# Loading k and q of the first two blocks as one pair of neighbouring tokens, in an attention and MLP kernel

## The chip, the cores and the metric

The kernel runs on one core of a Trainium2 chip. The metric is the device time of one launch in microseconds (us). Five things work side by side on a core: TensorE (PE in the profile, its weight loads PEld), VectorE (DVE), ScalarE (ACT), GpSimd (POOL) and SyncE (SP). SP, ACT and POOL also start transfers; the tables call those queues SPq, ACTq and POOLq.

## The reference

Attention with a sliding window of 128 keys and a bias that grows with distance, for 8 batches, 8 heads, 576 tokens, head size 64. Its result, seen as 4608 tokens of 512 features, goes through a two-layer MLP with squared ReLU.

```python
scores = scale * np.matmul(q, k.transpose(0, 1, 3, 2))
mask = (rel >= 0) & (rel < window)             # window = 128
scores = np.where(mask, scores + bias[None], -1000000000.0)
attn = np.exp(scores - np.max(scores, axis=-1, keepdims=True))
attn = attn / (np.sum(attn, axis=-1, keepdims=True) + 1e-09)
x = np.matmul(attn, v).transpose(0, 2, 1, 3).reshape(B * S, H * D)   # (4608, 512)
h = x @ w_in                                   # w_in (512, 2048)
out = np.maximum(h, 0.0) ** 2 @ w_out          # w_out (2048, 512)
```

## The kernel before

**Tiling.** Each batch of 576 tokens is cut into five blocks, four of 128 tokens and one of 64, so that there are 40 blocks, numbered through. A block goes through these steps: load k, q, v; turn k and q (transposes `tp` on PE, copied into a tile `kqT`); scores `ps_s` on PE; exponentials `E` on ACT (L598); the product with the masks, `P`, on DVE (L609); the values `pv` on PE (L639); the division on DVE (L662, L672), which gives `x`; the turn of `x` (`xp`, L698), copied into `xT`. From block 12 on (13 for `x`) the turns are DMA transposes.

The MLP takes groups of 512 tokens. Group 0 and group 1 use plain products `h` (L745), group 0 in four quarters of 128 tokens, the others a fast scheme of seven products in place of eight with sums of weights and tokens (`f`, L820; `o`, L979). `weight_sums` (L383 to L394) makes the sums of `w_in` that the scheme needs, in 32 DVE instructions of 256 columns.

**Order.** Nothing is ordered by hand. Each step is a task with an estimated duration for one or more engines, a key, its dependencies and the buffers that it takes and frees. `Plan.order` goes through all tasks as a list scheduler does and fixes which engine does which task and in what order. `SPREAD` shifts the keys of groups of tasks by random draws with fixed seeds, so that each list of draws gives another order of the whole program. Where the plan sees PE idle in its first 14 us, the last lines put small matmuls on `ident` there (L1127, L1129), which compute nothing that is used.

**The loads at the start.** All of k, q, v, w_in and w_out comes through POOL's queue, converted to bfloat16 on the way; `FIRST` (L221) gives the order: `b0` is the k, q, v of block 0, `i0` a quarter of the columns of w_in, `o0` a quarter of the rows of w_out. Only k and q of block 0 go another way (`load_block`, L405 to L424): as float32 into tiles `raw`, in halves of four heads, k by SP and q by ACT, one token a partition, so that a piece of 64 numbers (256 bytes) stands together in memory. A copy (`cast`) then converts each half. `prepare` turns block 0 in halves too: two transposes each of k and of q, and a copy of 256 columns after each two; the first half of block 0's scores (heads 0 to 3) needs only the first half of both.

Of the kernel before, what the change touches and what calls it, by code (L numbers as in the profile page):

```python
# [9 lines left out]
FP32 = mybir.dt.float32  # L10
BF16 = mybir.dt.bfloat16
# [190 lines left out]
def kernel(  # L202
    ctx: ExitStack, tc: tile.TileContext, q, k, v, moe_w_in, moe_w_out, out
):
    nc = tc.nc

    B, H, S, D = q.shape
# [10 lines left out]
    NG = NT // 512  # L218
    NBLK = B * NKB

    FIRST = "b0 b1 b2 i0 i1 b3 i2 b4 b5 i3 b6 o0 b7 b8 o1 o2 b9 o3"  # L221
    SPLIT = ([(0, 128), (128, 256), (256, 384), (384, 512)], [(0, 256), (256, 512)])

    KQ_DMA, X_DMA = 12, 13
# [158 lines left out]
    def weight_sums(n, key):  # L383
        w = w_in_sb.rearrange("p (c k) (j r f) -> p c r k j f", c=2, r=2, f=128)
        a11, a12, a21, a22 = (w[:, c, r, :, 2 * n:2 * n + 2] for r in range(2) for c in range(2))
        s1, s2, s3, s4 = (w_sum[:, i, :, 2 * n:2 * n + 2] for i in range(4))
        last = None
        for o, a, b, op in ((s1, a21, a22, ALU.add), (s2, s1, a11, ALU.subtract),
                            (s3, a11, a21, ALU.subtract), (s4, a12, s2, ALU.subtract)):
            def emit(o=o, a=a, b=b, op=op):  # L390
                for k in range(2):
                    nc.vector.tensor_tensor(o[:, k], a[:, k], b[:, k], op=op)
# [5 lines left out]
    def load_block(m, key):  # L398
        b, kb = divmod(m, NKB)
        n = blk[kb]  # L400
        s_in[m, "k"] = s_in[m, "q"] = Slot("kq")
        s_in[m, "v"] = Slot("v")
        for i, (nm, src) in enumerate((("k", k), ("q", q), ("v", v))):
            sl = s_in[m, nm]
            if m == 0 and nm != "v":  # L405
                st = Slot("osb")
                t_in[m, nm] = []
                for hf in range(2):
                    cols = slice(hf * 256, hf * 256 + 256)

                    def raw(src=src, st=st, nm=nm, hf=hf, cols=cols):
                        if not hf:
                            st.tile = work.tile([128, 512], FP32, tag="osb", bufs=plan.bufs["osb"], name="raw")
                        (nc.sync if nm == "k" else nc.scalar).dma_start(
                            st.tile[:, cols].rearrange("s (h d) -> s h d", d=D),
                            src[b, 4 * hf:4 * hf + 4, 0:n, :].rearrange("h s d -> s h d"))

                    def cast(i=i, st=st, sl=sl, nm=nm, hf=hf, cols=cols):
                        copy(t_in[0, nm][hf], kq[sl.idx][:, i, cols], st.tile[:, cols])
                    t_raw = plan.add({"SP" if nm == "k" else "ACT": 450.0}, -2e6 + hf, raw, [], [st],  # L420
                                     lat=(2490.0 if nm == "k" else 2860.0) + 650.0 * hf)
                    t_in[m, nm].append(plan.add({"DVE": 270.0, "ACT": 300.0}, key + 0.1 * hf + 0.01 * i, cast,
                                                [t_raw], [sl], [st]))
                continue  # L424

            def emit(i=i, src=src, sl=sl, nm=nm):
                o = (vt[sl.idx][0:n, :, 0:D] if nm == "v"
                     else (kq[sl.idx][0:n, i] if n == 128 else kq[sl.idx][i * n:i * n + n, 0]).rearrange("s (h d) -> s h d", h=H))
                nc.gpsimd.dma_start(o, src[b, :, kb * 128:kb * 128 + n, :].rearrange("h s d -> s h d"))  # L429
            t_in[m, nm] = load(key + 0.01 * i, 920.0 if n == 128 else {"k": 550.0, "q": 300.0, "v": 550.0}[nm], emit, [t_ones] + (t_zeros if m >= NKB - 1 else []) if nm == "v" else [], [sl])  # L430

    for i, what in enumerate(FIRST.split()):
        {"b": load_block, "i": load_w_in, "o": load_w_out}[what[0]](int(what[1:]), -9e5 + i)
    for m in range(2 * NKB, NBLK):
        load_block(m, -5e5 + m)

# [4 lines left out]
    def copy(task, o, i):  # L441
        if task.eng == "DVE":
            nc.vector.tensor_copy(o, i)
        else:
            nc.scalar.activation(o, i, AF.Copy)

    def prepare(m):
# [5 lines left out]
        kq_by_dma = m >= KQ_DMA  # L453


        sk = sk_of[m] = Slot("kqT")
        if kq_by_dma:
            def turn_kq():
                src = kq[s_in[m, "k"].idx]
# [251 lines left out]
    m = 0  # L711
# [246 lines left out]
    def product(g, i, key):  # L958
# [13 lines left out]
        for j, x in ([(j, x) for x in range(len(parts)) for j in range(FCB // 2)] if halves  # L972
                     else [(j, x) for j in range(FCB // 2) for x in range(len(parts))]):
                t, lo, hi = parts[x]

                def emit(j=j, x=x, t=t, lo=lo, hi=hi):
                    if opens and j == 0 and (x == 0 or apart):
                        bank[x].tile = bank_tile(bank[x], "o")
                    nc.tensor.matmul(bank[x].tile[:, t * 256 + lo:t * 256 + hi],  # L979
                                     left(g, what, j)[:, t * 128:(t + 1) * 128], right(by, j)[:, lo:hi],  # L980
                                     start=opens and j == 0 and (x == 0 or apart), stop=j == FCB // 2 - 1,
                                     skip_group_check=True)
                t = x
                new = j == 0 and t == 0
                here = [bank[t]] if opens and j == 0 and (t == 0 or apart) else []
                end = i == 6 and j == FCB // 2 - 1 and t == len(parts) - 1
                if what[0] == "s":
                    needs = [t_sum[g, j // 4]]
                else:
                    needs = [q for lo, hi, q in g_sq[g][2 * j + (what != "a11")]]  # L990
                last = plan.add({"PE": mm(hi - lo)}, key(i * 16 + 2 * j + min(t, 1)), emit,
                                [last, (t_wmix if by[0] == "t" else t_wout)[j // 2], kp["t"][where] if new else None] + needs,
                                here, [g_slots[g], s_slots[g][0]] if end else [s_slots[g][1]] if i == 1 and j == FCB // 2 - 1 and t == 1 else [])
                if j == FCB // 2 - 1:
                    done_at.append(last)
# [166 lines left out]
```

## Time and profile before

| what | us |
|---|---|
| median of three runs (lowest, highest) | 291.88 (290.7, 292.52) |
| the profiled execution's own time | 291.28 |
| its span, first to last instruction | 289.4 |
| PE busy in the span | 281.4 |
| DVE busy | 256.4 |
| ACT busy | 228.8 |
| POOL busy | 107.7 |

The span is what the views of the profile divide up; the 1.88 us beyond it lie outside the instructions. The time of a launch is read against the median. The granted TensorE clock was 1.00 throughout. PE is busy 97% of the span, so what is looked for is the 8 us in which it isn't, and matmuls that do nothing useful.

### The profile page before, as it was taken

The numbers are of one execution on the slowest core, as the hardware profiler recorded it, in microseconds if no ns is written. First come the engines' busy times: TensorE is split into PE (matmuls) and PEld (weight loads), VectorE is DVE, ScalarE is ACT, GpSimd is POOL, SyncE is SP. The second block draws the span as 40 slices with busy tenths as digits, with TensorE's granted clock in tenths as the row PEclk, the third lists the DMA queues.
The fourth block names the chain that finished last, engine by engine and source line by source line (L and its number), as shares of the span: only waits on it lengthen the run. The fifth ranks groups of instructions, "written<-read, shape, count | busy, mean of one in ns | idle before, by whom it ended". The sixth has DMA issues, their size and how long they took to land.

```text
span 289.4 us, 9511 instructions
## 1 busy us (share of the span) xinstructions
PE 281.4 (97%) x3879; PEld 239.5 (83%) x3885; DVE 256.4 (89%) x627; ACT 228.8 (79%) x470; POOL 107.7 (37%) x134
## 2 busy tenths in 40 slices
PE   8899999999999999999999999999999999999995
PEld 6788878865788888888888898888888888888894
DVE  6867779999798999998999999989999988998823
ACT  6659788995489985999899989898879888588420
POOL 8958676844644437322734245332000000000000
PEclk9999999999999999999999999999999999999999
DMA  9999999999999999999999999999234111201223
GB/s 135 161 181 162 173 177 180 155 137 178 173 155 151 187 176 179 153 170 126 209 145 137 138 198 139 162 170 179 35 100 72 46 21 59 88 0 39 74 75 109
DMA packets 166011, 38.36 MB, mean 133 GB/s; under 512 B 153040, under 2 KB 165456, under 8 KB 165968
## 3 DMA queue, kind: packets, MB, share of 16 engines
q0 software_dynamic: 114704, 18.10, 91.0%
q1 hardware_dynamic: 50208, 19.41, 37.6%
q8 instruction: 30, 0.49, 0.7%
q10 hardware_dynamic: 1056, 0.26, 0.4%
q14 instruction: 13, 0.11, 0.1%
HBM read 36.70 MB, written 9.44 MB: 159 GB/s over the span
## 4 chain that ended last, share of the span: by engine, by line
PE 86%; DMA 5%; POOL 3%; DVE 2%; ACT 2%; issue 0%; DVEq 0%; ACTq 0%
PE o L979 33%; PE f L820 30%; PE h L745 7%; PE pv L639 5%; DMA w_in_sb<-in_moe_w_in_dram 5%; PE o L1059 5%; PE ps_s L533 3%; POOL vt L429 1%; POOL kq L429 1%; PE tp L483 1%; PE ps_s L552 1%; PE xp L698 1%; ACT rt L759 1%; DVE rt L854 1%; ACT E L591 0%
## 5 line engine op out<-in xcount | busy, mean ns | idle before, releaser
L598 ACT ACTIVATE E<-ps_s 128x384 bf16<-128x384 f32 (+2 forms) x114 | 50.5, 507 | 8.6 <-PE ps_s L533 8.6
L429 POOL DMA_DIRECT2D vt<-in_v_dram x40 | 34.0, 851 | 58.6 <-PE pv L639 50.1
L979 PEld LDWEIGHTS <-g 128*128 128x128 bf16 x512 | 49.0, 98 | 6.0
L820 PEld LDWEIGHTS <-w_sum 128*128 128x128 bf16 x448 | 43.2, 98 | 6.3 <-issue 0.3
L609 DVE TENSOR_TENSOR P<-E,masks 128x1024 bf16<-128x1024 bf16 (+1 forms) x67 | 43.5, 657 | 2.5 <-ACT E L598 1.6
L429 POOL DMA_DIRECT2D kq<-in_k_dram x39 | 33.1, 849 | 32.4 <-DMA kqT<-kq 25.4
L979 PEld LDWEIGHTS <-S 128*128 128x128 bf16 x400 | 37.0, 98 | 4.3 <-issue 0.4
L848 ACT ACTIVATE rt<-f 128x512 bf16<-128x512 f32 x56 | 33.2, 598 | 6.8 <-PE f L820 6.6
L979 PE MATMUL o<-w_out_sb,g 128*128 128x256 bf16 x256 | 38.4, 273 | 0.0
L979 PE MATMUL o<-w_mix,g 128*128 128x256 bf16 x256 | 37.2, 273 | 0.0
L745 PE MATMUL h<-xT,w_in_sb 128*128 128x128 bf16 (+1 forms) x384 | 35.5, 237 | 1.2 <-DMA w_in_sb<-in_moe_w_in_dram 0.7
L979 PE MATMUL o<-w_mix,S 128*128 128x256 bf16 (+1 forms) x264 | 36.1, 269 | 0.2 <-ACT E L598 0.2
L820 PEld LDWEIGHTS <-w_in_sb 128*128 128x128 bf16 x336 | 31.7, 98 | 4.4
L820 PE MATMUL f<-xT,w_in_sb 128*128 128x256 bf16 x224 | 34.6, 273 | 0.0
L429 POOL DMA_DIRECT2D kq<-in_q_dram x39 | 33.3, 853 | 2.5 <-DMA w_out_sb<-in_moe_w_out_dram 1.4
L871 ACT ACTIVATE g<-rt 128x512 bf16<-128x512 bf16 x52 | 32.6, 635 | 1.7 <-DVE rt L859 0.9
L820 PE MATMUL f<-xT,w_sum 128*128 128x256 bf16 x224 | 33.5, 272 | 0.2 <-DVE rt L854 0.2
L672 DVE TENSOR_TENSOR x<-pv,rec 128x256 bf16<-128x256 f32 (+1 forms) x80 | 33.1, 415 | 0.4
L820 PE MATMUL f<-T,w_sum 128*128 128x256 bf16 x224 | 32.1, 273 | 0.0
L639 PE MATMUL pv<-vt,P 128*128 128x65 bf16 x576 | 30.8, 193 | 0.9 <-DVE P L609 0.9
L639 PEld LDWEIGHTS <-P 128*128 128x128 bf16 x576 | 25.8, 97 | 6.1 <-DVE P L609 2.2
L745 PEld LDWEIGHTS <-w_in_sb 128*128 128x128 bf16 x384 | 26.7, 98 | 4.2 <-DMA w_in_sb<-in_moe_w_in_dram 1.9
(78 smaller groups left out, 503.1 us busy)
## 6 DMA issues: line engine op xcount, KB each, us to landing
out_dram<-osb SPq DMA_DIRECT2D x35, 256.0 KB, 3.8
vt<-in_v_dram POOLq DMA_DIRECT2D x32, 128.0 KB, 6.2
kq<-in_k_dram POOLq DMA_DIRECT2D x31, 128.0 KB, 6.5
kq<-in_q_dram POOLq DMA_DIRECT2D x31, 128.0 KB, 6.9
w_out_sb<-in_moe_w_out_dram POOLq DMA_DIRECT2D x4, 512.0 KB, 9.6
w_in_sb<-in_moe_w_in_dram POOLq DMA_DIRECT2D x6, 256.0 KB, 8.5
kq<-in_k_dram POOLq DMA_DIRECT2D x8, 64.0 KB, 5.6
kq<-in_q_dram POOLq DMA_DIRECT2D x8, 64.0 KB, 5.8
```

What stands on the lines that cost most here:

```text
L429: nc.gpsimd.dma_start(o, src[b, :, kb * 128:kb * 128 + n, :].rearrange("h s d -> s h d"))
L533: nc.tensor.matmul(sl.tile[lo:lo + 64, at:at + w], k[rows, c, unit:unit + 64], own[rows, C + c, q0:q0 + w], start=True, stop=True)
L598: nc.scalar.activation(o, src, AF.Exp, bias=0.0, scale=scale)
L609: nc.vector.tensor_tensor(Pt[sP.idx][:, hs, p0:2, 0:n], e, masks[:, hs, p0:2, 0:n], op=ALU.mult)
L639: nc.tensor.matmul(slot_v.tile[:, hi * (D + 1):(hi + 1) * (D + 1)], Pt[sP.idx][:, place(h), part, :], vt[s_in[mk, "v"].idx][:, h, :], star ...
L672: nc.vector.tensor_tensor(xt[sx.idx][0:n, hf * 256:(hf + 1) * 256].rearrange("p (h e) -> p h e", h=4), pv[0:n, :, 0:D], srec.tile[0:n, :]. ...
L745: nc.tensor.matmul(slot.tile[:, f * w:(f + 1) * w], w_in_sb[:, cc, (fc + f) * 128:(fc + f + 1) * 128], xT[:, cc, g * 512 % RING + lo:g * 5 ...
L820: nc.tensor.matmul(bank[name].tile[:, jj * 256:jj * 256 + 256], w, m, start=opens and jj == 0 and k == 0, stop=k == 1, skip_group_check=True)
L848: nc.scalar.activation(srt.tile, bank[name].tile, AF.Relu, bias=0.0, scale=1.0)
L871: nc.scalar.activation(o, i, AF.Square)
L979: nc.tensor.matmul(bank[x].tile[:, t * 256 + lo:t * 256 + hi], left(g, what, j)[:, t * 128:(t + 1) * 128], right(by, j)[:, lo:hi], start=o ...
L1059: nc.tensor.matmul(bank.tile, g_slots[g].tile[:, fc, t * 128:(t + 1) * 128], w_out_sb[:, fc], start=fc == 0, stop=fc == FCB - 1)
```

## The change

1. k and q of blocks 0 and 1 (256 tokens) are loaded as one pair (`load_pair`), unconverted, k by SP and q by ACT. Partition p holds tokens 2p and 2p + 1, so that 128 numbers (512 bytes) stand together. There are still two halves of four heads, so four transfers as before, each of twice the bytes. The two loads of k and q of block 1 leave POOL's queue. v of block 0 is loaded first there, then block 2, then v of block 1 (`FIRST`); the plan puts it ahead of v of block 2.
2. Four casts of 512 columns, for two blocks, take the place of four of 256, for one. The plan may give them to ACT too.
3. Four groups of four transposes turn both blocks: each transpose takes 128 columns of even or of odd tokens. Eight copies of 256 columns bring even and odd tokens back into order (x = 0 for block 0, x = 1 for block 1), where six copies were (four of 256, two of 512).
4. `weight_sums` makes each sum in one instruction of 2 x 256 columns in place of two of 256: 16 instructions for 32.
5. The key of the last group's products uses `t` where it used `min(t, 1)`.
6. `SPREAD` has other seeds, so that the whole order is drawn anew.

```diff
-    FIRST = "b0 b1 b2 i0 i1 b3 i2 b4 b5 i3 b6 o0 b7 b8 o1 o2 b9 o3"
+    FIRST = "r0 v0 b2 v1 i0 i1 b3 i2 b4 b5 i3 b6 o0 b7 b8 o1 o2 b9 o3"
+    PAIRS = (0,)
...
             def emit(o=o, a=a, b=b, op=op):
-                for k in range(2):
-                    nc.vector.tensor_tensor(o[:, k], a[:, k], b[:, k], op=op)
-            last = plan.add({"DVE": 2 * dve(256, 2)}, key, emit, [t_win[n][-1], last, t_read[1][0]])
+                nc.vector.tensor_tensor(o, a, b, op=op)
+            last = plan.add({"DVE": dve(512, 2)}, key, emit, [t_win[n][-1], last, t_read[1][0]])
...
+    def load_pair(m, key):
+        b, kb = divmod(m, NKB)
+        for i, (nm, src) in enumerate((("k", k), ("q", q))):
+            sl = s_in[m, nm] = s_in[m + 1, nm] = Slot("kq")
+            t_in[m, nm] = t_in[m + 1, nm] = []
+            for hf in range(2):
+                st = Slot("osb" if nm == "k" else "fu")
+
+                def raw(src=src, st=st, nm=nm, hf=hf):
+                    st.tile = work.tile([128, 512], FP32, tag=st.tag, bufs=plan.bufs[st.tag], name="raw")
+                    (nc.sync if nm == "k" else nc.scalar).dma_start(
+                        st.tile.rearrange("p (h e) -> p h e", e=2 * D),
+                        src[b, 4 * hf:4 * hf + 4, kb * 128:kb * 128 + 256, :].rearrange("h (p u) d -> p h (u d)", u=2))
+
+                def cast(j=len(t_in[m, nm]), st=st, sl=sl, nm=nm, hf=hf):
+                    copy(t_in[m, nm][j], kq[sl.idx][:, :, hf * 256:hf * 256 + 256].rearrange("p u (h d) -> p u h d", d=D),
+                         st.tile.rearrange("p (h u d) -> p u h d", u=2, d=D))
...
-                    t_in[m, nm].append(plan.add({"DVE": 270.0, "ACT": 300.0}, key + 0.1 * hf + 0.01 * i, cast,
-                                                [t_raw], [sl], [st]))
...
+        if m in PAIRS:
...
+            for hf, j, nm in ((hf, j, nm) for hf in range(2) for j, nm in enumerate("kq")):
...
+                for i in range(C):
+                    def emit(i=i, nm=nm, hf=hf, slot=slot, alloc=alloc):
...
+                        c, u = divmod(i, 2)
+                        c += 2 * hf
+                        nc.tensor.transpose(slot.tile[:, i * 128:(i + 1) * 128],
+                                            kq[s_in[m, nm].idx][:, u, c * 128:(c + 1) * 128], ident)
...
+                for x in range(2):
+                    def evac(x=x, y=len(t_kq_of[m]) - x, j=j, hf=hf, slot=slot):
+                        lo = j * C + 2 * hf
+                        o = kqT[sk_of[m + x].idx][:, lo:lo + 2, :].rearrange("p c (i u) -> p c i u", u=2)
+                        copy(t_kq_of[m + x][y], o,
+                             slot.tile[:, 0:512].rearrange("p (c u i) -> p c i u", c=2, u=2)[:, :, 64 * x:64 * x + 64, :])
...
-                last = plan.add({"PE": mm(hi - lo)}, key(i * 16 + 2 * j + min(t, 1)), emit,
+                last = plan.add({"PE": mm(hi - lo)}, key(i * 16 + 2 * j + t), emit,
...
-    SPREAD = ((78, 3, 1), (425, 16, 0.01), (451, 8, 0.01), (463, 8, 0.03), (537, 3, 0.1), (602, 1.5, -0.15),
-              (705, 3, 0.03), (1454, 16, 0.03), (1463, 3, -0.15), (1578, 3, 0.03), (1611, 3, 0.01))
+    SPREAD = ((12129, 3, 1), (12200, 16, 0.03), (12228, 3, 0.1), (12268, 8, 0.01), (12289, 8, 0.03),
+              (12340, 8, 0.01), (12399, 3, 0.1), (12433, 8, 0.03), (12492, 3, 0.01), (12507, 3, 0.1),
+              (12666, 3, 0.03))
```

What the scheduler makes of it is seen in the program's order. First POOL's queue, the loads at the start (`vt` is a tile of v, `kq` one of k and q; the first row is block 0 in both). Before:

```order
L429 DMA vt_75<-in_v_dram 128x8x64
L429 DMA kq_71<-in_k_dram 128x8x64
L429 DMA kq_71<-in_q_dram 128x8x64
L429 DMA vt_76<-in_v_dram 128x8x64
L429 DMA kq_73<-in_k_dram 128x8x64
L429 DMA kq_73<-in_q_dram 128x8x64
L429 DMA vt_77<-in_v_dram 128x8x64
L360 DMA w_in_sb<-in_moe_w_in_dram 128x2x512 x4
```

And now:

```order
L433 DMA vt_75<-in_v_dram 128x8x64
L433 DMA kq_71<-in_k_dram 128x8x64
L433 DMA kq_71<-in_q_dram 128x8x64
L433 DMA vt_76<-in_v_dram 128x8x64
L433 DMA vt_77<-in_v_dram 128x8x64
L361 DMA w_in_sb<-in_moe_w_in_dram 128x2x512 x4
```

Five loads stand ahead of the first piece of w_in where seven did; behind it the queue is the same up to the last piece of w_in.

Second ACT, from its first mask to the exponentials of block 0 (`kqT_0` and `kqT_1` are the turned k and q of blocks 0 and 1, `E_0` the exponentials of block 0). Before:

```order
L332 ACTIVATE masks_65<-dist_137 128x256 x8
L445 ACTIVATE kqT_0_81<-tp_180 128x256
L598 ACTIVATE E_0_90<-ps_s_185 128x256
L598 ACTIVATE E_0_90<-ps_s_186 128x256
L598 ACTIVATE E_0_90<-ps_s_195 128x256
L598 ACTIVATE E_0_90<-ps_s_198 128x256
```

And now:

```order
L333 ACTIVATE masks_65<-dist_137 128x256 x3
L449 ACTIVATE kq_2_73<-raw_100 128x2x256
L333 ACTIVATE masks_65<-dist_137 128x256 x3
L449 ACTIVATE kq_2_73<-raw_141 128x2x256
L333 ACTIVATE masks_65<-dist_137 128x256 x2
L449 ACTIVATE kqT_1_82<-tp_174 128x256
L449 ACTIVATE kqT_0_81<-tp_174 128x256
L449 ACTIVATE kqT_1_82<-tp_186 128x256
L449 ACTIVATE kqT_0_81<-tp_186 128x256
L449 ACTIVATE kqT_1_82<-tp_163 128x256
L637 ACTIVATE E_0_90<-ps_s_196 128x256
L637 ACTIVATE E_0_90<-ps_s_197 128x256
```

Both casts of q and five of the eight copies now stand on ACT ahead of block 0's exponentials; before, one copy did.

Third DVE, from block 0's first values to the copy that opens block 1's tokens to the MLP (`rec` and `x` are the division, `P` the masked exponentials, `xT` the turned x). In the change:

```order
L701 RECIPROCAL rec_275<-pv_268 128x4
L447 COPY kqT_2_83<-tp_204 128x1024
L711 TENSOR_TENSOR x_0_87<-pv_268,rec_275 128x256
L701 RECIPROCAL rec_337<-pv_279 128x4
L648 TENSOR_TENSOR P_1_86<-E_1_91,masks_65 128x1024
L711 TENSOR_TENSOR x_0_87<-pv_279,rec_337 128x256
L648 TENSOR_TENSOR P_1_86<-E_1_91,masks_65 128x1024
L701 RECIPROCAL rec_368<-pv_343 128x4
L648 TENSOR_TENSOR P_0_85<-E_2_92,masks_65 128x1024
L711 TENSOR_TENSOR x_1_88<-pv_343,rec_368 128x256
L701 RECIPROCAL rec_402<-pv_372 128x4
L648 TENSOR_TENSOR P_0_85<-E_2_92,masks_65 128x1024
```

Before, the first `xT` copy stood on DVE ahead of both `P` of block 1, and the copy into `kqT_2` was ACT's; now DVE does that copy, and the first `xT` copy is ACT's, between two exponentials of block 2.

More of the change, by code (lines that the diff above doesn't have):

```diff
@@ L390, in emit @@
             def emit(o=o, a=a, b=b, op=op):
-                for k in range(2):
-                    nc.vector.tensor_tensor(o[:, k], a[:, k], b[:, k], op=op)
-            last = plan.add({"DVE": 2 * dve(256, 2)}, key, emit, [t_win[n][-1], last, t_read[1][0]])
+                nc.vector.tensor_tensor(o, a, b, op=op)
+            last = plan.add({"DVE": dve(512, 2)}, key, emit, [t_win[n][-1], last, t_read[1][0]])
         t_wsum[n] = last
     s_in, t_in = {}, {}
-    def load_block(m, key):
+    def load_pair(m, key):
[13 more added lines that the diff above has]
+                         st.tile.rearrange("p (h u d) -> p u h d", u=2, d=D))
+                t_raw = plan.add({"SP" if nm == "k" else "ACT": 450.0}, -2e6 + hf, raw, [], [st],
+                                 lat=(2700.0 if nm == "k" else 3000.0) + 900.0 * hf)
+                t_in[m, nm].append(plan.add({"DVE": dve(512), "ACT": act(512) + 42.0}, key + 0.1 * hf + 0.01 * i, cast,
+                                            [t_raw], [sl] if hf == 0 else [], [st]))
@@ L399, in load_block @@
+    def load_block(m, key, only="kqv"):
         b, kb = divmod(m, NKB)
         n = blk[kb]
-        s_in[m, "k"] = s_in[m, "q"] = Slot("kq")
+        if "k" in only:
+            s_in[m, "k"] = s_in[m, "q"] = Slot("kq")
         s_in[m, "v"] = Slot("v")
         for i, (nm, src) in enumerate((("k", k), ("q", q), ("v", v))):
+            if nm not in only:
+                continue
             sl = s_in[m, nm]
[L405 to L421, printed above, removed]
-                    t_in[m, nm].append(plan.add({"DVE": 270.0, "ACT": 300.0}, key + 0.1 * hf + 0.01 * i, cast,
-                                                [t_raw], [sl], [st]))
-                continue
@@ L432 @@
     for i, what in enumerate(FIRST.split()):
-        {"b": load_block, "i": load_w_in, "o": load_w_out}[what[0]](int(what[1:]), -9e5 + i)
+        {"r": load_pair, "v": functools.partial(load_block, only="v"), "b": load_block, "i": load_w_in, "o": load_w_out}[what[0]](int(what[1:]), -9e5 + i)
     for m in range(2 * NKB, NBLK):
```

20 lines of the change are left out of this document (added).

## The prediction

> **What bounds the kernel now.** I read the table by stage first, then PE's waits, then what PE waits for. The stages are cut at PE's first product `h` (13.78), at the landing of the last piece of w_in (31.02) and at the last matmul (285.98):
>
> ```profile
> core 0: us, PE busy (x) PEld busy (x) DVE busy (x) ACT busy (x) POOL busy (x), PEclk, DMA share, GB/s
> 0.00:4.00 4.00, 2.94 (x28) 2.90 (x28) 2.24 (x13) 2.12 (x4) 3.19 (x8) 1.00 0.56 123
> 4.00:8.00 4.00, 3.43 (x36) 2.21 (x33) 3.45 (x11) 3.22 (x12) 4.00 (x6) 1.00 2.25 149
> 8.00:13.78 5.78, 4.89 (x133) 4.22 (x133) 4.74 (x15) 3.50 (x8) 5.78 (x8) 1.00 1.65 164
> 13.78:31.02 17.24, 16.03 (x316) 14.21 (x314) 12.41 (x30) 13.31 (x30) 12.19 (x16) 1.00 1.81 170
> 31.02:285.98 254.96, 254.15 (x3374) 215.93 (x3380) 233.21 (x560) 206.68 (x421) 82.51 (x99) 1.00 1.26 129
> 285.98:289.40 3.42, 0.00 (x0) 0.00 (x0) 0.29 (x1) 0.00 (x0) 0.00 (x0) 1.00 0.43 144
> ```
>
> From 31.02 to 285.98 PE lacks 254.96 - 254.15 = 0.81 us of being busy throughout. That stage is nine tenths of the span and set by PE's own work, which the change leaves alone: the same matmuls but for the fillers on `ident`. The last 3.42 us are the final stores, untouched. What an edit at the start can win lies ahead of 31.02. There PE waits for weights:
>
> ```profile
> PEld L745 <- DMA w_in_sb<-in_moe_w_in_dram: 1.9, 5, 0.9
> 15.67 0.34 PEld L745 LDWEIGHTS <-w_in_sb 128*128 128x128 bf16 x6 [0.27 <-DMA w_in_sb<-in_moe_w_in_dram]
> 17.19 0.28 PEld L745 LDWEIGHTS <-w_in_sb 128*128 128x128 bf16 x5 [0.38 <-DMA w_in_sb<-in_moe_w_in_dram]
> 22.32 1.23 PEld L745 LDWEIGHTS <-w_in_sb 128*128 128x128 bf16 x22 [0.19 <-DMA w_in_sb<-in_moe_w_in_dram]
> 23.75 0.10 PEld L745 LDWEIGHTS <-w_in_sb 128*128 128x128 bf16 x1 [0.20 <-DMA w_in_sb<-in_moe_w_in_dram]
> 31.02 0.28 PEld L745 LDWEIGHTS <-w_in_sb 128*128 128x128 bf16 x5 [0.86 <-DMA w_in_sb<-in_moe_w_in_dram]
> ```
>
> Each row is a group of weight loads, and the bracket says how long the engine stood ahead of it. Five times PE has used up what has landed of w_in; the last stop, at 31.02, is the longest. The chain that ended last says the same, with two transfers in it:
>
> ```profile
> 8.28 7.35 DMA w_in_sb<-in_moe_w_in_dram
> 22.98 7.99 DMA w_in_sb<-in_moe_w_in_dram
> ```
>
> They land at 15.63 and 30.97, each nearly 8 us after its issue: the queue ahead of them is full. So two things race to 31 us, the stream of loads and PE's work on the first blocks.
>
> **The stream of loads.** POOL's queue loses two loads of block 1 and the unconverted ones double:
>
> ```profile
> 2.38 0.89 POOL L429 DMA_DIRECT2D kq<-in_k_dram  x1
> 3.26 0.90 POOL L429 DMA_DIRECT2D kq<-in_q_dram  x1
> 16.16 0.69 POOL L429 DMA_DIRECT2D kq<-in_k_dram  x1 [1.60 <-DMA w_in_sb<-in_moe_w_in_dram]
> kq<-in_k_dram POOLq DMA_DIRECT2D x31, 128.0 KB, 6.5
> w_in_sb<-in_moe_w_in_dram POOLq DMA_DIRECT2D x1, 512.0 KB, 8.0
> raw<-in_q_dram ACTq DMA_DIRECT2D x2, 128.0 KB, 3.7
> raw<-in_k_dram SPq DMA_DIRECT2D x2, 128.0 KB, 3.4
> GB/s 0 0 23 123 146 172 156 146 159 184 248 284 284 269 264 266 294 284 284 287 287 281 254 218 179 168 164 161 155 155 143 120 106 127 151 137 143 149 148 149
> ```
>
> Block 1's k and q cost POOL 0.89 + 0.90 = 1.8 us of issue. At 16.16 POOL itself waits for a landing before it can issue more, so an earlier landing passes on to all later issues. What they cost the stream: from the landing that ends the stop at 23.75 to the one at 30.97 there came k, q, v of block 4 (64 KB each), of block 5 (128 KB each) and 512 KB of w_in, 1088 KB in 7.22 us, or 151 KB a us. Two loads of 128 KB are then **1.7 us**. The unconverted loads grow from 4 x 128 to 4 x 256 KB; no transfer of 512-byte pieces stands in the trace. If the number of pieces decides (4 x 512, as before), the extra is nothing; if the bytes decide, it is 512 KB at the 284 GB/s that the last row shows from 1.6 to 5.6 us while these loads run, 1.85 us. I take **0.6 us**, nearer to the pieces: the loads through POOL move smaller pieces at half that rate, so pieces cost. The last piece of w_in then lands at 30.97 - 1.7 + 0.6 = 29.9 us, with bounds of 29.3 and 31.1.
>
> [...]
>
> **PE's work on the first blocks.** The new order puts more on ACT ahead of block 0's exponentials, so I go along its chain with the durations of before:
>
> ```profile
> 3.17 2.56 ACT L332 ACTIVATE masks<-dist 128x256 bf16<-128x256 f32 x8
> 6.51 0.38 ACT L445 ACTIVATE kqT<-tp 128x256 bf16<-128x256 bf16 x1 [0.78 <-PE tp L483]
> 6.79 1.21 ACT L598 ACTIVATE E<-ps_s 128x256 bf16<-128x256 f32 x4
> 9.92 1.64 ACT L598 ACTIVATE E<-ps_s 128x384 bf16<-128x384 f32 x4 [1.43 <-PE ps_s L533]
> 13.32 1.64 ACT L598 ACTIVATE E<-ps_s 128x384 bf16<-128x384 f32 x4 [0.85 <-PE ps_s L533]
> L445 ACT ACTIVATE osb<-o 128x512 f32<-128x512 f32 x14 | 8.5, 610 | 6.2 <-PE o L1059 4.7 <-PE o L979 1.4
> 5.02 1.00 DVE L443 CAST kq<-raw 128x256 bf16<-128x256 f32 x2
> 11.21 1.29 DVE L609 TENSOR_TENSOR P<-E,masks 128x1024 bf16<-128x1024 bf16 x2 [0.36 <-ACT E L598]
> 8.71 0.42 DVE L672 TENSOR_TENSOR x<-pv,rec 128x256 bf16<-128x256 f32 x1
> 8.49 0.18 DVE L662 RECIPROCAL rec<-pv 128x4 f32<-128x4 f32 x1
> 20.70 0.69 DVE L443 COPY kqT<-tp 128x1024 bf16<-128x1024 bf16 x1
> 13.83 1.28 PE L745 MATMUL h<-xT,w_in_sb 128*128 128x128 bf16 x16
> 17.43 0.27 PEld L698 LDWEIGHTS <-x 128*128 128x128 bf16 x4
> ```
>
> A mask is 2.56 / 8 = 0.32 us, a copy of 256 columns 0.30 to 0.38, a cast of 512 columns on ACT I take from the copy of that size, 0.6. Three masks end at 4.1, the first cast of q at 4.9, three masks at 5.9; the second half of q, whose cast on DVE was under way by 5.5 (the second of the two from 5.02), is now due at about 5.9, so its cast ends at 6.5, two masks at 7.15, five copies at 8.65. Block 0's exponentials, which ran at 6.79 to 8.00, now run at 8.65 to 9.85, **1.9 us later**; block 1's end at 11.5, which is where they ended before (11.56), and three of block 2's at 12.7, where before they only began at 13.32. What is late next is DVE: from 10.2 on, reciprocal, `kqT_2` copy, division, reciprocal, `P`, division add up to 0.18 + 0.69 + 0.42 + 0.18 + 0.65 + 0.42 = 2.5 us, then four PE transposes (0.4) and ACT's copy (0.6) open block 0's tokens at 13.6; the first `h` stood at 13.83. The two `P` of block 2 end on DVE at 15.3, block 1's division at 15.7, and with 34 `h` done PE turns block 2's `x` at about 17.35. Before, it did so at 17.43 with 37 `h` done, of which 16 take 1.28 us without stops. Gain 0.08, loss 3 x 0.06: **nothing** by this stage, with bounds of 0.6 earlier (the second half of q by 5.3, as before) and 2.7 later (casts and copies across two strides at twice the time, 2 x 0.6 + 5 x 0.3).
>
> **The sum.** With the same work behind it, PE would come to the last piece of w_in at 31.02 less the three stops after 17.43: 0.19 + 0.20 + 0.86 = 1.25, at 29.8. The piece lands at 29.9. So the later of the two decides: 31.02 - 29.9 = **-1.1 us**.
>
> The sums of w_in lie elsewhere:
>
> ```profile
> L392 DVE TENSOR_TENSOR w_sum<-w_in_sb x16: 253/283/286, 47.9 to 70.5; 128x256 bf16<-128x256 bf16 x16
> L377 DVE TENSOR_TENSOR w_mix<-w_out_sb 128x512 bf16<-128x512 bf16 x8 | 3.2, 414 | 0.0
> 40.00:60.00 20.00, 19.95 (x325) 16.43 (x323) 18.61 (x62) 18.10 (x37) 15.35 (x19) 1.00 1.97 167
> 60.00:80.00 20.00, 19.68 (x257) 13.11 (x258) 17.83 (x50) 12.81 (x30) 10.34 (x13) 1.00 1.96 165
> ```
>
> One of 512 columns takes 0.41 where two of 256 (0.28 each, the middle number) take 0.56, so DVE saves 16 x 0.15 = 2.4 us, between 48 and 71 us. PE hides it: it lacks 0.05 and 0.32 us there, so the gain is between 0 and 0.37, and I take 0. If the form over two pieces runs at half rate it costs DVE some 4 us in a stretch where it is 91% busy, still under PE. The key with `t` in place of `min(t, 1)` acts in the last group alone, whose products form one chain in any case: 0.
>
> The new draws change the order of everything after 31 us. At best they save the 0.81; at worst every 20 us is like 60:80, the worst stretch of before, 12.7 x 0.32 = 4.1 us in place of 0.81, so +3.3. I take 0, since the same planner makes both orders from the same costs.
>
> Sum: the profiled time of 291.28 - 1.1 = 290.2. The median of the runs lies 0.6 above the profiled time, so **290.8 us**.
>
> **The rivals.**
>
> *ACT's chain turns late (slower).* If the casts and copies with two strides take twice as long, block 0's exponentials start 2.7 us later, and all that hangs on them; PE comes to w_in's last piece at 29.8 + 2.7 = 32.5, 1.5 us later than now: 293.4. It decides once the chain is over 1.25 us late. For it: ACT's chain has no slack there, and none of these forms is in the trace. Against: contiguous copies take 0.3 to 0.4 us.
>
> *The new order costs more after 31 us (slower).* Up to +3.3 on the forecast, 294.1. For it: each block's exponentials, masks and squares share ACT and DVE at 81% and 91% of that stage. Against: PE stood only 0.81 us in all of 255.
>
> *The new order and the start both come out well.* The last piece lands at 29.3 and the start is 0.6 early, so -1.7 there, and -0.81 after: 291.88 - 2.5 = 289.4, and less if the pace between stops, which no row prices, improves as well.
>
> *The transfers only trade places.* At the price of the bytes in full the last piece lands at 31.1, at two thirds of it at 30.5, so the end moves by +0.1 to -0.5 us: 291.4 to 292.0, and the change does not do what it says to the stream. For it: the extra 512 KB pass through the same engines. Against: they come in pieces no more numerous than before. [...]
>
> **How the numbers follow.** A measurement of this kernel can tell about 1%, 2.9 us, from no change. Forecast 0.40 (its own range 289.8 to 292.0), late ACT 0.17, costlier order 0.15, all well 0.18, traded places 0.10. Faster by over 1%, below 288.96: most of the all-well case, which I widen for the unpriced pace (0.16), and 0.02 of the forecast: 0.18. Slower by over 1%, above 294.8: 0.09 of the costlier order and 0.06 of the late ACT: 0.15. Within 1%: 0.67. The range runs from 288.7 (all well with some pace) to 294.0 (the costlier order, near its full price).
>
> **What would show it.** Right: w_in's last piece lands near 29.9 and PE's stop ahead of it is under 0.3 us; PEld's waits for w_in fall from 1.9 to under 0.7; block 0's exponentials start at 8 to 9 us, yet the first `h` stays within 0.5 us of 13.8; PE lacks about 0.8 us after that. Wrong: the second halves of `raw` landing after 6.5 us, ACT's strided copies above 0.5 us, a first `h` after 15, or over 2 us of stops on PE after 31.

## The result: 290.1 us, and where the profile changed

The changed kernel takes 290.10 us (median of 11 runs, 289.58 to 291.18) where the kernel before takes 291.55 (11 runs, 290.70 to 292.52) on the same chip. The ratio is 0.9955, with an interval of 0.9936 to 0.9973. The forecast was 290.8. The profiled execution of the change took 289.83 us, with a span of 288.1 where before had 289.4.

One sentence above is wrong: the description of the change says that the plan puts v of block 1 ahead of v of block 2 on POOL's queue. `vt_76` is block 2's (PE's values of block 1 wait for the load behind it), so v of block 2 comes first, as `FIRST` has it. No number hung on it.

The last three stages of the kernel after, cut at the same events: PE's first `h` (14.00), the landing of the last piece of w_in (28.5) and the last matmul (284.63).

```profile
core 0: us, PE busy (x) PEld busy (x) DVE busy (x) ACT busy (x) POOL busy (x), PEclk, DMA share, GB/s
14.00:28.50 14.50, 14.22 (x298) 13.14 (x296) 10.63 (x30) 11.53 (x24) 10.71 (x14) 1.00 1.90 176
28.50:284.63 256.13, 255.54 (x3401) 216.17 (x3399) 233.83 (x545) 208.22 (x426) 82.92 (x100) 1.00 1.30 129
284.63:288.10 3.47, 0.00 (x0) 0.00 (x0) 0.29 (x1) 0.00 (x0) 0.00 (x0) 1.00 0.43 142
```

The last matmul ends 1.35 us earlier (285.98 before), and the stores behind it take what they took, 3.47 against 3.42. So the whole gain lies ahead of the last matmul. Between the first `h` and w_in's landing PE now lacks 14.50 - 14.22 = 0.28 us; before it lacked 17.24 - 16.03 = 1.21. After the landing it lacks 0.59, where before it lacked 0.81.

What PE and its weight loads waited for at `h` (us in all, times, longest), and the groups behind these sums (the bracket is the idle time ahead of the group; "issue" means that the profile names no releaser):

```profile
PEld L784 <- issue: 0.9, 2, 0.6
PE h L784 <- issue: 0.4, 1, 0.4
PEld L784 <- DMA w_in_sb<-in_moe_w_in_dram: 0.3, 1, 0.3
22.53 0.56 PEld L784 LDWEIGHTS <-w_in_sb 128*128 128x128 bf16 x10 [0.33 <-DMA w_in_sb<-in_moe_w_in_dram]
28.68 0.82 PEld L784 LDWEIGHTS <-w_in_sb 128*128 128x128 bf16 x14 [0.27 <-issue]
35.01 0.45 PEld L784 LDWEIGHTS <-w_in_sb 128*128 128x128 bf16 x8 [0.61 <-issue]
```

Of the five stops for w_in, 1.9 us in all, one of 0.33 is left, and the one ahead of the last piece is gone. Two stops without a named releaser stand in their place; the longer one shows on the matmuls' row too, as 0.4.

The loads: POOL's issue of the first and of the last pieces of w_in, the time from issue to landing of the last one, and the unconverted loads.

```profile
5.84 2.89 POOL L361 DMA_DIRECT2D w_in_sb<-in_moe_w_in_dram  x4
20.36 0.75 POOL L361 DMA_DIRECT2D w_in_sb<-in_moe_w_in_dram  x1
w_in_sb<-in_moe_w_in_dram POOLq DMA_DIRECT2D x1, 512.0 KB, 8.1
raw<-in_q_dram ACTq DMA_DIRECT2D x2, 256.0 KB, 4.9
raw<-in_k_dram SPq DMA_DIRECT2D x2, 256.0 KB, 4.4
```

The last piece is issued at 20.36 and lands 8.1 us later, at 28.5. Before it landed at 30.97. The last half of q lands at 6.85, seen in the chain that ended last, whose transfers are now these:

```profile
1.25 5.60 DMA raw<-in_q_dram
12.27 10.22 DMA w_in_sb<-in_moe_w_in_dram
```

PE's path into the blocks, in order: the two casts on ACT, the five copies, the exponentials of blocks 0 to 2, then PE's first `h` and the turn of block 2's `x`; last the sums of w_in by duration (lowest, middle, highest).

```profile
5.02 0.63 ACT L449 ACTIVATE kq<-raw 128x512 bf16<-128x512 f32 x1 [0.83 <-DMA raw<-in_q_dram]
6.87 0.63 ACT L449 ACTIVATE kq<-raw 128x512 bf16<-128x512 f32 x1 [0.31 <-DMA raw<-in_q_dram]
8.02 1.46 ACT L449 ACTIVATE kqT<-tp 128x256 bf16<-128x256 bf16 x5
9.34 3.96 ACT L637 ACTIVATE E<-ps_s 128x256 bf16<-128x256 f32 x11
14.00 0.44 PE L784 MATMUL h<-xT,w_in_sb 128*128 128x128 bf16 x5
17.00 0.39 PE L737 MATMUL xp<-ident,x 128*128 128x128 bf16 x4
L392 DVE TENSOR_TENSOR w_sum<-w_in_sb x8: 414/416/417, 42.6 to 64.4; 128x512 bf16<-128x512 bf16 x8
```

ACT's chain turns 2.55 us late (9.34 against 6.79), but the first `h` moves only by 0.17 (14.00 against 13.83), and block 2's `x` is turned 0.48 earlier (its weight loads start at 16.95 against 17.43).

Behind the start PE has no gap left in the three stretches where it had one before. First the two of before that stand nowhere above (the third is 60:80, with 19.68 of 20), then the three of now:

```profile
80.00:100.00 20.00, 19.81 (x273) 16.90 (x271) 18.50 (x44) 18.12 (x37) 10.33 (x12) 1.00 1.77 164
160.00:180.00 20.00, 19.82 (x282) 17.15 (x280) 19.92 (x49) 18.37 (x40) 8.76 (x11) 1.00 1.74 160
```

```profile
60.00:80.00 20.00, 20.00 (x266) 13.30 (x264) 16.75 (x41) 12.91 (x29) 9.25 (x11) 1.00 1.95 173
80.00:100.00 20.00, 20.00 (x282) 16.84 (x284) 18.49 (x44) 18.20 (x38) 10.34 (x12) 1.00 1.83 158
160.00:180.00 20.00, 20.00 (x263) 17.27 (x262) 19.71 (x46) 17.68 (x38) 7.70 (x9) 1.00 2.03 177
```

PE being busy doesn't say that it does something useful, so I also counted useful work: all weight loads up to a time but those of the fillers, each with PE's time for its kind of product, in both traces. By 31 us the change is 1.4 us of work ahead (20.35 against 18.93), by 40 us 0.7 (28.81 against 28.09), by 50 us 0.65 (38.90 against 38.25). That count is mine and good to a few tenths. The other 0.7 of the 1.35 comes after 50 us, where before has its gaps of 0.32, 0.19 and 0.18. All of this rests on one profiled execution of each kernel.

So the result has two halves, the start and the order after it. The experiments take them apart.

### The profile page after: what moved, and what is told of

The parts are those of the page before. It is cut to its first block, busy times and chain, and to the rows that moved or that the text cites. A ratio compares the mean times of both kernels' runs of the same rounds, so it can differ in the third digit from the quotient of the medians.

```text
span 288.1 us, 9479 instructions
## 1 busy us (share of the span) xinstructions
PE 281.2 (98%) x3878; PEld 238.4 (83%) x3878; DVE 254.2 (88%) x606; ACT 230.7 (80%) x477; POOL 105.8 (37%) x132
## 4 chain that ended last, share of the span: by engine, by line
PE 91%; DMA 5%; ACT 1%; POOL 1%; DVE 0%; issue 0%; ACTq 0%
PE o L1018 34%; PE f L859 30%; PE h L784 8%; PE pv L678 6%; PE o L1098 5%; DMA w_in_sb<-in_moe_w_in_dram 4%; PE ps_s L572 3%; DMA raw<-in_q_dram 2%; PE ps_s L591 2%; PE tp L522 1%; PE xp L737 1%; ACT kqT L449 0%; POOL vt L433 0%; DVE P L648 0%; POOL w_in_sb L361 0%
## 5 line engine op out<-in xcount | busy, mean ns | idle before, releaser
L433 POOL DMA_DIRECT2D kq<-in_k_dram x38 | 32.2, 848 | 26.9 <-DMA kqT<-kq 20.9
L1018 PE MATMUL o<-w_out_sb,g 128*128 128x256 bf16 x256 | 39.2, 273 | 0.0
L1018 PE MATMUL o<-w_mix,g 128*128 128x256 bf16 x256 | 38.9, 273 | 0.0
L1018 PE MATMUL o<-w_mix,S 128*128 128x256 bf16 (+1 forms) x264 | 37.8, 269 | 0.0
L910 ACT ACTIVATE g<-rt 128x512 bf16<-128x512 bf16 x57 | 35.5, 633 | 1.6 <-DVE rt L898 0.7
L859 PE MATMUL f<-xT,w_in_sb 128*128 128x256 bf16 x224 | 35.5, 273 | 0.0
L433 POOL DMA_DIRECT2D kq<-in_q_dram x38 | 32.4, 853 | 2.1 <-DMA w_in_sb<-in_moe_w_in_dram 1.3
L859 PE MATMUL f<-T,w_sum 128*128 128x256 bf16 x224 | 33.1, 273 | 0.0
L678 PE MATMUL pv<-vt,P 128*128 128x65 bf16 x576 | 29.5, 194 | 0.1
L678 PEld LDWEIGHTS <-P 128*128 128x128 bf16 x576 | 24.1, 97 | 5.7 <-DVE P L648 2.5
```

The costliest lines, as they stand in the source:

```text
L678: nc.tensor.matmul(slot_v.tile[:, hi * (D + 1):(hi + 1) * (D + 1)], Pt[sP.idx][:, place(h), part, :], vt[s_in[mk, "v"].idx][:, h, :], star ...
L859: nc.tensor.matmul(bank[name].tile[:, jj * 256:jj * 256 + 256], w, m, start=opens and jj == 0 and k == 0, stop=k == 1, skip_group_check=True)
L910: nc.scalar.activation(o, i, AF.Square)
```

## The experiments

Each is compared with the kernel before, run on the same chip as the experiment. Its median there was 291.48 us for e1 to e4, 291.54 for e5 to e7 and 291.08 for e8 to e10. My theory was that of the prediction: the pair takes two loads out of the stream ahead of w_in, and the new order is neutral. The rivals: the order does it, or something else at the start.

### The draws alone, and the pair alone

**e1, the change with the draws of before:**

```diff
-    SPREAD = ((12129, 3, 1), (12200, 16, 0.03), (12228, 3, 0.1), (12268, 8, 0.01), (12289, 8, 0.03),
...
+    SPREAD = ((78, 3, 1), (425, 16, 0.01), (451, 8, 0.01), (463, 8, 0.03), (537, 3, 0.1), (602, 1.5, -0.15),
```

> The changed kernel with the random draws (SPREAD) of the kernel before. Theory (the pair shortens the stream of loads, and PE gets w_in earlier): the gain stays, 290.0 to 291.0 us against 291.5 of before, w_in's last piece lands at 28 to 29 us as with the change (28.5), against 31.0 before. Rival (the new draws made the gain): 291.3 us or more, although w_in lands early; then PE stands over 1 us longer after 31 us.

Measured: 294.73 us, ratio 1.0112 (1.0092 to 1.0133). **e2, the kernel before with the new draws** (the same edit the other way round):

> The kernel before with the draws of the change, nothing else. Theory (the stream of loads): no gain, 291.0 to 293.5 us, w_in's last piece still lands at 30.5 to 31.5 us. Rival (the draws): 290.0 to 290.6 us.

Measured: 296.82 us, ratio 1.0188 (1.0169 to 1.0207). Both mixtures are slower than both pure kernels. The time of e1 is the rival's, that of e2 is outside both expectations. The loss lies in the middle, not at the start. Two stretches and a wait of e1, then the worst stretch of e2 and its longest wait in the middle:

```profile
100.00:120.00 20.00, 18.81 (x269) 15.72 (x267) 19.19 (x45) 16.40 (x36) 9.94 (x13) 1.00 1.78 176
160.00:180.00 20.00, 19.02 (x273) 15.97 (x272) 19.04 (x44) 17.35 (x35) 8.57 (x10) 1.00 1.57 162
PE f L859 <- ACT fu L929: 1.3, 2, 1.0
```

```profile
100.00:120.00 20.00, 18.37 (x265) 15.12 (x263) 18.52 (x43) 15.82 (x34) 9.43 (x12) 1.00 1.80 178
PE f L820 <- DVE x L672: 1.3, 1, 1.3
```

In e1 PE waits there for ACT's copies of partial products (`fu`), in e2 for a division on DVE (`x`); such stretches cost 1 to 1.6 us each. Draws that fit one program cost 4.6 us (294.73 - 290.1) or 5.3 us (296.82 - 291.5) when the program around them is another.

The same seeds aren't the same order, though. The numbers are drawn for one group of tasks after another, and the two programs' lists of groups differ (2,085 and 2,084 groups, 2,082 of them in both), so that 660 of the 2,082 get another shift from the same seed. What e1 and e2 show is the price of an order that was picked for neither program; they don't put the one kernel's order on the other.

The start of e1 is as good as that of the change: no stop for w_in, its last piece issued at 20.52 and landed 7.8 later, at 28.3.

**e6 and e7, no draws at all**, before and the change with `SPREAD = ()`:

> The kernel before with no random draws at all (SPREAD empty). Both theories: slower than its own draws, by some 5 us as the foreign draws were (296.8): 295 to 299 us, the loss after 80 us, where PE waits for ACT and DVE.

> The changed kernel with no random draws. Theory (the pair is worth about 1 us at the start, whatever the order after it): by 40 us PE has done about 1 us more of its work than the kernel before without draws; the whole time is 0 to 3 us below that kernel's, the spread being what the order after 40 us adds. Rival (only fitted draws make the gain): no less work missing at 40 us, equal or slower.

Measured: e6 292.64 us, ratio 1.0041 (1.0026 to 1.0057), e7 293.91, ratio 1.0089 (1.0071 to 1.0107). So draws are worth 1.1 us to the kernel before and 3.8 to the change; I had looked for far more in the first, and for e7 to end up to 3 us ahead of e6. By the count of work, e7 is 1.4 us ahead of e6 at 50 us, and ends 1.3 us behind it. This stretch and these waits of e7 say where that went:

```profile
140.00:160.00 20.00, 18.44 (x258) 15.59 (x257) 19.73 (x48) 16.59 (x35) 7.42 (x10) 1.00 1.46 140
PE f L859 <- ACT fu L929: 1.4, 1, 1.4
PE f L859 <- ACT fx L940: 1.1, 3, 0.5
```

The pair's start is ahead in every order tried (0.65 to 1.4 us by 50 us), but whether anything of it is left at the end is decided by the order behind it.

### The sums alone

**e4, the kernel before with sums 512 columns wide:**

```diff
-                for k in range(2):
-                    nc.vector.tensor_tensor(o[:, k], a[:, k], b[:, k], op=op)
+                nc.vector.tensor_tensor(o, a, b, op=op)
```

> The kernel before, in its own order, with each sum of w_in as one instruction over 2 x 256 columns; the planner's costs are those of before, so nothing moves. Theory: DVE saves 16 x 0.15 = 2.4 us and the time stays within 0.4 us of 291.5, since PE covers it. Rival (DVE, 91% busy there, holds PE up): 0.5 to 1.5 us less, 290.0 to 291.0.

Measured: 291.59 us, ratio 1.0003 (0.9984 to 1.0023). DVE does each in 0.418 us where two took 0.56, and the end doesn't move by more than the interval, 0.6 us to either side. But its profile showed something else:

```profile
22.80 1.18 PEld L744 LDWEIGHTS <-w_in_sb 128*128 128x128 bf16 x21 [0.65 <-issue]
35.64 1.01 PEld L744 LDWEIGHTS <-w_in_sb 128*128 128x128 bf16 x18 [1.07 <-issue]
L391 DVE TENSOR_TENSOR w_sum<-w_in_sb x8: 386/418/420, 48.1 to 70.5; 128x512 bf16<-128x512 bf16 x8
```

In this execution w_in's last piece landed 1.6 us earlier than in that of before (issued at 22.41, landed 7.0 later, 29.4 against 30.97), and there was no stop for w_in at all. Yet the time is the same: two stops without a releaser, 1.72 us, stood in its place. By the count of work e4 is 0.7 us ahead of before at 31 us and 0.3 behind at 35.5; between them lies its stop of 1.07. The stop at 31.02, on which my prediction leaned most, is then not the one thing that sets the start's end.

### The two loads put back

**e3** puts two loads of the size of block 1's k and q back into POOL's queue of the change, right behind v of block 0, ahead of block 2. Their data is used by nothing.

```diff
+                if m == 0 and nm == "v":
+                    for j, more in enumerate((k, q)):
+                        spare = w_mix[:, j].rearrange("p j n -> p (j n)")[:, 0:d_model]
+                        nc.gpsimd.dma_start(spare.rearrange("s (h d) -> s h d", h=H),
+                                            more[0, :, 128:256, :].rearrange("h s d -> s h d"))
```

> The changed kernel in its own order on every engine, with two more loads in POOL's queue behind v of block 0: k and q of block 1 once more, into a place that is written over later and not read before. Theory (the stream): w_in's last piece lands 1.7 to 2.5 us later, at 30.2 to 31.0, PE's stops for w_in grow from 0.6 to 2 or more us, and the time goes to 291.0 to 292.0 us, all of the gain lost. Rival (the start on ACT and DVE, or the order): within 0.3 us of 290.1.

Measured: 292.00 us, ratio 1.0015 (1.0001 to 1.0029), 1.9 us slower than the change: the whole gain is gone, but by another road. No stop for w_in came back. PE stood for block 2's k, which comes two loads later, and by 25 us it was 2.1 us of work behind the change. Its wait, and the group behind it:

```profile
PE tp L527 <- DMA kq<-in_k_dram: 1.4, 1, 1.4
9.73 0.34 PEld L527 LDWEIGHTS <-kq 128*128 128x128 bf16 x4 [1.69 <-DMA kq<-in_k_dram]
```

**e5** puts the same two loads behind block 2 and the v of block 1, right ahead of the first piece of w_in, so that only w_in comes late (`if n == 0 and i == 0:` in the loader of w_in, then the same lines).

> The changed kernel in its own order, the two loads of k and q of block 1 put back into POOL's queue right ahead of w_in's first piece, behind all loads of blocks 0 to 2, so that block 2 isn't late; what they load isn't used. Theory (w_in's landing sets the pace to 31 us): no stop at block 2's turn, w_in's last piece at 30.2 to 31.0 us in place of 28.5, PE's stops for w_in 2 us or more, 291.0 to 292.0 us. Rival (w_in lands early enough to spare, and what counted was block 2's k and q alone): within 0.4 us of 290.1.

Measured: 290.43 us, ratio 0.9969 (0.9956 to 0.9981). POOL issues the first piece of w_in at 7.74 (5.84 in the change, 7.59 before) and the last at 22.81:

```profile
7.74 2.84 POOL L366 DMA_DIRECT2D w_in_sb<-in_moe_w_in_dram  x4
w_in_sb<-in_moe_w_in_dram POOLq DMA_DIRECT2D x1, 512.0 KB, 6.7
PEld L789 <- DMA w_in_sb<-in_moe_w_in_dram: 0.8, 2, 0.4
```

The last piece lands at 29.5, 1.0 later than in the change, stops of 0.8 us for w_in are back, and the median is 0.33 us higher, as the rival had it. The intervals of the two ratios don't tell that from nothing; they allow from -0.2 to 1.1 us. So little is left at the end of what I had given as the whole cause. It isn't little at 31 us: by the count of work the change is 0.8 to 0.9 us ahead of e5 from 28 to 34 us, and 0.2 at 35. In between stands the change's stop at 35.01, and e5 has none there.

What e3 loses, it has lost before w_in's last piece is due. It hangs on the loads of block 2, which in the change come earlier by two loads and one of v. POOL's issue of its k, q and v (with v of block 1) there:

```profile
2.37 0.89 POOL L433 DMA_DIRECT2D kq<-in_k_dram  x1
3.25 0.89 POOL L433 DMA_DIRECT2D kq<-in_q_dram  x1
4.11 1.78 POOL L433 DMA_DIRECT2D vt<-in_v_dram  x2
```

And of its k and q in the kernel before:

```profile
4.99 0.91 POOL L429 DMA_DIRECT2D kq<-in_k_dram  x1
5.86 0.92 POOL L429 DMA_DIRECT2D kq<-in_q_dram  x1
```

### Both kernels fitted anew

**e8 and e9**: do the two halves of the result survive if both kernels get draws chosen in the same way? The draws were picked from none, for each kernel alone, by the end that its own planner gives.

```diff
-    SPREAD = ((12129, 3, 1), (12200, 16, 0.03), (12228, 3, 0.1), (12268, 8, 0.01), (12289, 8, 0.03),
...
+    SPREAD = ((40002, 3, 0.1), (40006, 8, 0.03), (40011, 1.5, 0.03), (40014, 1.5, 0.03), (40018, 3, 0.03),
...
```

> The changed kernel with other draws, picked afresh from none by the end that the kernel's own planner gives (some 1,700 draws looked at). Theory A (the pair gives 0.65 to 1.4 us by 50 us, and an order fitted to it loses nothing behind): within 0.6 of the changed kernel's 290.1, so 289.5 to 290.7. Theory B (the good run of the changed kernel after 50 us is luck of its eleven draws, as the foreign draws of 294.7 were bad luck): 291.0 to 294.0.

> The kernel before with other draws, picked in the same way (some 1,900 draws looked at). Theory A (the pair itself is worth about 1 us once each order is fitted): 0.7 to 1.8 us behind the pair fitted in the same way of the same call, so 290.6 to 291.8. Theory B (the difference between the two kernels is that of their draws alone): within 0.5 us of the pair fitted in the same way.

Measured: e8 290.57 us, ratio 0.9958 (0.9927 to 0.9989); e9 291.34, ratio 0.9999 (0.9978 to 1.0021). Each comes back to within 0.5 us of the kernel whose program it shares, with quite other draws. The pair is ahead by 0.77 us in the medians and 0.0041 in the ratios, 1.2 us. That is at the edge of what these runs can tell from nothing: the two intervals taken together just do, but the runs themselves overlap (288.63 to 291.76 and 289.88 to 292.69). So the pair is worth some 1 us once each order is fitted, if it is worth anything beyond the noise, and a good order for it is no accident of eleven draws. By the count of work e8 is 1.5 us ahead of e9 at 50 us. Neither is better than the change, which stays the best version measured.

e8 has room: its twelve runs spread from 288.63 to 291.76, and the profiled one, at the slow end, shows PE standing for a turn by DMA that came late:

```profile
60.00:80.00 20.00, 18.69 (x280) 12.13 (x279) 16.44 (x40) 11.28 (x26) 9.26 (x11) 1.00 1.78 144
76.66 0.23 PEld L591 LDWEIGHTS <-kqT 64*128 64x128 bf16 x8 [1.43 <-DMA kqT<-kq]
```

Whether that wait is what separates its runs wasn't tried.

### The stops without a releaser

**e10** moves the work against the count of weight loads: eight more matmuls ahead of the first transposes, where PE waited 1.10 us for k. Does such a stop stand at a count, or at a place in the work?

```diff
-        for _ in range(28):
+        for _ in range(36):
```

> The changed kernel with 36 instead of 28 matmuls ahead of the first transposes, where TensorE had 1.10 us free; its order behind them is the same. The changed kernel's weight loads stopped at 28.68 (0.27 us) and 35.01 (0.61 us) with nothing that the profile names as releaser. [...] Theory B (the stop belongs to the place in the work): 28.7 and 35.0, ahead of the same matmuls of h. Time 290.1, 0.3 to either side, by both.

Measured in one run: 289.89 us, span 288.1, as the change. Its stops:

```profile
21.96 1.01 PEld L784 LDWEIGHTS <-w_in_sb 128*128 128x128 bf16 x18 [0.28 <-issue]
28.30 1.24 PEld L784 LDWEIGHTS <-w_in_sb 128*128 128x128 bf16 x22 [0.41 <-issue]
34.59 0.90 PEld L784 LDWEIGHTS <-w_in_sb 128*128 128x128 bf16 x16 [0.59 <-issue]
```

Counted from the start of the trace, 351, 479 and 606 weight loads stand ahead of these three. In the change 479 and 606 stand ahead of its two, and 351 ahead of the one at 22.53 that the profile gives to w_in. In e4 the two stood at 351 and 606. So the stop keeps its count while the work under it moves by eight matmuls, and the times move with it (28.68 to 28.30, 35.01 to 34.59). For a stop that keeps its count I had expected 27.8 and 34.2; the shift is half of that, and what eight matmuls of `h` take, 8 x 0.056 = 0.45 us. It isn't the place in the work that stops. e9 shows it in other work altogether, at counts 223 and 351:

```profile
16.46 0.10 PEld L639 LDWEIGHTS <-P 128*128 128x128 bf16 x1 [1.13 <-issue]
23.21 0.11 PEld L533 LDWEIGHTS <-kqT 64*64 64x64 bf16 x2 [0.73 <-issue]
```

## Why the prediction was right, and by which steps it was not

The time, the sign and the range were right. The sum had one term that counted, -1.1 at the start, and the span moved by -1.35; but the parts are not all the ones that I had named. The start gave 1.3 to 1.4 and kept 0.65 of it, and the order gave 0.7 that I had put at nothing: that the total came out near is in part luck. The 0.6 that the sum adds for the median was taken from three runs; over eleven runs before's median is 0.27 above its profiled time. So 290.8 stands 0.7 above the measured time, although the medians differ by only 0.35 us more than forecast (1.45 for 1.1).

**What bounds the kernel** was right: a stage bound by PE's own work, a tail that doesn't move (3.47 against 3.42), and a start that can win about a microsecond.

**The stream of loads** was mis-sized. Predicted was a landing of w_in's last piece at 29.9, between 29.3 and 31.1; it came at 28.5, 2.5 us earlier, outside the bounds. Over all profiles the five with the queue of the change (it, e1, e7, e8, e10) land it at 28.3 to 28.5, and the five with the queue of before (it, e2, e4, e6, e9) at 29.4 to 31.0; the 30.97 that I counted from is the latest of these. Two loads put back give 29.5 (e5) and 30.3 (e3). So the two loads cost 1.0 to 1.8, for which I had 1.7. The term that failed is the price of the doubled `raw`, +0.6: e5 and e3 issue as many loads on POOL as before, and carry 512 KB more beside them, and their last piece lands no later than in the kernels before. The price is seen at the head of the queue alone. The first load through POOL, v of block 0, lands at 7.5 to 8.1 us in every kernel with the pair and at 6.0 to 6.3 in those without, some 1.4 us later. At the eighth load, w_in's first piece, nothing is left of that: 13.5 in e3 and e5, 13.4 to 14.0 with the queue of before. What makes it up in between isn't shown. The row of bytes moved from 1.6 to 5.6 us, here for the kernel after:

```profile
GB/s 0 0 36 123 108 87 108 138 174 189 189 230 271 297 302 302 317 353 354 338 338 338 333 369 343 333 338 348 333 312 307 282 297 282 307 271 307 276 282 243
```

It stands at 333 to 369 for 1.2 us, where before stood at 264 to 294 for 1.1. The two rows don't compare the pieces alone: in these 4 us POOL's queue moved 42 packets of 2,069 in the change, and 1,596 of 3,708 before.

**"The later of the two decides"** was the step that made the sum, and it was true in a way that I hadn't priced. With the landing at 28.5, PE itself is the later of the two, at my 29.8, which would be -1.2; by 31 us PE was 1.4 us of work ahead. But by 40 us 0.7 of that was gone. Counted every quarter of a us, the lead is 1.1 to 1.3 from 31 to 34.5 us and 0.6 from 35 on. The stop at 35.01 (0.61 us) lies just there; it comes by count of weight loads and was in none of my terms. So a landing 1.0 later costs e5 0.9 us of work at 31 us, near to what the prediction held, and 0.33 at its end; e5 meets no such stop.

**PE's path into the blocks**, for which I took 0, was right in its sum and wrong in its parts. The casts took 0.63 (0.6 expected) and the strided copies no more than the contiguous ones, five in 1.46 us where one took 0.38 before. The second half of q came 0.95 later than I had it (6.85 against 5.9), and one sign of being wrong that I had named, second halves that land after 6.5, came for q (that of k landed at 6.19). Block 0's exponentials began at 9.34, not 8.65, outside my 8 to 9. It cost nothing, since the stretch behind it has its cover: the first `h` at 14.00 (13.6 expected, 13.7 by its own terms; within 0.5 of 13.8 as asked). What I missed there is block 2: its k and q leave POOL 2.6 us earlier, and PE turned its `x` at 16.95 where I had 17.35. e3 shows that path without cover: k of block 2 late by two loads stops PE for 1.4 us, and the end is 1.9 us later.

**The sums of w_in**: 0, by DVE's 0.416 where I had 0.41 (e4 shows the zero alone). **The key with `t`**: not tried apart.

**The new draws**, for which I took 0 "since the same planner makes both orders from the same costs", was the second step that failed. At its place in the change the new order is worth about -0.7: PE's gaps after 50 us are gone. Its upper bound, +3.3, was too low: foreign draws cost 4.6 and 5.3 us (e1, e2), since I had taken the worst 20 us of one fitted order as the worst of any.

**The rivals.** *ACT's chain turns late* came true in its first half, 2.55 us late, and didn't decide: its price of 1.5 us let PE idle where it had other work. *The new order costs more* is what e1 is, 294.7 beside 294.1 in the text; it didn't occur with draws made for this program. *All well* is nearest to what took place: gaps after 31 us gone and an earlier landing, but with half of the landing lost again. *The transfers only trade places* is out: the extra bytes cost w_in nothing.

What stays open: whether the stop at 35.01 stands in every execution of the change, and what the change would take without it. No run takes it away alone, and only one execution of each kernel was traced.

## What to carry to other kernels

Take apart the start and the order behind it before you price a change to a program that a planner orders: the same edit was worth -1.4 us with draws made for it, some -1 with both sides fitted alike (at the edge of the noise), and +3.2 with seeds chosen for another program. A landing that comes earlier was worth here only what the engine's own path left (0.33 us at the end for 1.0 of landing, e5 against the change): look for what is late next, here the loads of the block after the one that the change was made for, and then the stops of TensorE by count. Twice the bytes, in larger pieces on two other queues, cost the first load of POOL's queue 1.4 us and w_in nothing (last piece at 29.5 and 30.3 in e5 and e3, 29.4 to 31.0 with the queue of before), so moving loads off that queue paid (28.3 to 28.5).

## What the runs showed of the hardware

I had not expected TensorE's stops at a fixed count of weight loads. They stand at 223, 351, 479 and 606 weight loads, 128 apart but for the last, which is 127 on in all seven runs that stop there. They last 0.3 to 1.1 us and stand in the first 38 us, and not each execution has them: before, e1, e5 and e7 show none. (Not each "issue" on the row of the weight loads is one. In e2 such a row of 0.41 stands at 28.23, and its matmuls wait for DVE by their own row. At the stops of e9 the matmuls' rows name no releaser either.) The page of every kernel also has this queue:

```profile
q8 instruction: 30, 0.49, 0.7%
```

30 packets in 0.49 MB are 16.4 KB each, and the trace holds when each of them moved. At the two stops of the change, and for comparison at a count at which the kernel before doesn't stop (us):

| run, weight loads ahead | packet has moved | next weight load | between | stop |
|---|---|---|---|---|
| change, 479 | 27.14 | 28.68 | 1.54 | 0.27 |
| change, 606 | 33.72 | 35.01 | 1.29 | 0.61 |
| before, 606 | 33.52 | 35.22 | 1.70 | none |

The row of DMA doesn't set the first 38 us apart, since it reads full up to 215 us. What makes the stops wasn't shown, nor whether these packets have a part in them: the profile names no releaser, and no run moved the packets themselves.

Strides cost ACT nothing in these forms: a copy of 256 columns that brings even and odd tokens together took 0.383 us in the mean of five, the one of contiguous columns before 0.38.

```profile
L449 ACT ACTIVATE kqT<-tp 128x256 bf16<-128x256 bf16 x5 | 1.5, 383 | 0.0
```
